# q in two shifted copies, turned in 32x32 blocks on VectorE: one attention and mixture-of-depths kernel, before and after

## The chip, the cores and the metric

The kernel runs on one core of one Trainium2 chip. The metric is the device time of one execution in microseconds. Before the change three runs gave 207.98, 209.22 and 209.74 us; their median, 209.22 us, is the time before. A profiled execution is a separate run of its own: it took 210.15 us, of which the span from the first to the last instruction is 208.4 us.

## What is computed

The reference has two parts. The first is linear attention over 8 batches, 8 heads, 576 tokens and a head size of 64, all in fp32:

```
q_s = softmax(q) over the 64 features of a token
k_s = softmax(k) over the 576 tokens
kv  = k_s^T v                    # 64 x 64 for each batch and head
x   = q_s kv                     # heads put side by side: 576 x 512 for each batch
```

The second part scores each token (`x . w_gate`), takes the 128 best of each batch, sends them through `relu(xe w1) w2` (512 to 1024 to 512), and adds the result, times the sigmoid of the score, to these rows. All other rows of the output are x itself.

## The kernel before, in words

**Units.** A unit is one batch and four heads, so there are 16 units, two for each batch. Each unit loads q, k and v (0.59 MB each), takes exp of q and k, sums `kv` over the tokens (`kv_mm`, line 310, made ready by `kv_out`), turns q (`q_t`, line 349) and multiplies (`x_mm`, line 375). A token's own softmax sum is one more column of that product. `x_sums` takes its reciprocal and a column with the score, `x_scale` writes the scaled rows into `xs`, and `x_store` writes them to the output.

**How q lies.** A partition holds nine neighbouring tokens: partitions 0 to 63 those of heads 0 and 2, partitions 64 to 127 those of heads 1 and 3 (heads 0 and 2 make one pair, 1 and 3 the other). The product needs the features on the partitions, so `q_t` turns q on TensorE: one transpose takes 64 tokens by two heads, and 18 of them turn a unit, ten in `q_t(u, 0)` (token rows 0 to 4 of each partition) and eight in `q_t(u, 1)` (rows 5 to 8). They land in PSUM, and one copy on ScalarE and one on VectorE (lines 356 and 354) take them to `qT`. Units 0 to 2 use a wider form, nine transposes of 128x128 (line 342).

**Rows of x.** `x_mm(u, 0)` makes the rows of the first pair of heads, `x_mm(u, 1)` those of the second, in five rounds each. A round writes token rows 0 to 4 to partitions 0 to 63 and rows 5 to 8 to partitions 64 to 127. There are nine rows, so the fifth round has real results for the lower partitions alone; the upper ones are filled with bf16 products of ones (line 367), so that the sums and the scale can run over all 128 partitions.

**The second part.** When both units of a batch are done, `score` and `score_row` make a row with all scores, `compare` (line 446, five times, on VectorE) counts for each token how many tokens score higher, `hits` marks the ranks below 128, `find` (line 473) turns the marks into row numbers, and `fetch` gathers these rows of x from the output by an indirect DMA on POOL (line 487). `turn` (line 524) transposes them, `mlp1` (line 544) and `mlp2` (line 554) are the two dense products in eight pieces each, `finish` adds, and `put` scatters the rows back (line 559).

**The order of work.** Everything is issued in an order written out by hand. After a start of its own, the loop has one step `s` per unit. A step handles unit `s` to its store, sums `kv` of unit `s + 1`, takes exp of q of unit `s + 1` and of k of unit `s + 2`, copies v of unit `s + 2`, and puts eight MLP pieces between these: odd steps `mlp1`, even steps `mlp2`, for an earlier batch. Each engine works through its own queue in that order. In even steps the search (`find`, `fetch`) comes after one MLP piece (two in step 16; in step 4 it stands further back), and `turn` stands before the last piece.

**Queues.** Loads and stores go through SP's queue: in step `s` the store of unit `s`, then k, v and q of unit `s + 3`, each into one of three buffers. The first load of a step waits for the last product of `x_mm(s, 1)`. A hardware DMA also waits, in the built program, for the landing of the one that was issued eight before it. Gathers and scatters go through POOL.

Of the kernel before, what the change touches and what calls it, by code (L numbers as in the profile page):

```python
# [8 lines left out]
F32 = mybir.dt.float32  # L9
# [8 lines left out]
def kernel(  # L18
# [34 lines left out]
    SD = S * D  # L53
    NQ = H // 4
    C = D + 2
    G = 2 * R
    LOW = 2.0 ** -30
    FAR = 2.0 ** 100
    UP = 2.0 ** 24
# [29 lines left out]
    def part(i):  # L89
        return slice(64 * i, 64 * i + 64)  # L90
# [10 lines left out]

    LD = 3
    FLAT = 0, 1
    RR = 4 * R
    raw = {w: [const.tile([P, 2 * T if w == "q" else RR, D], F32, name=f"{w}{n}") for n in range(LD)] for w in "qkv"}

    def view(t, paired):
        return t.rearrange("p (h r) d -> p h r d", h=4) if paired else t[:, :2 * T].rearrange("p (i r) d -> p i r d", i=2)
# [6 lines left out]
    def load(u, which, after=None, split=False, flat=False):  # L115
        b, qd = units[u]
        for what in which:
            src = {"q": q, "k": k, "v": v}[what]
            first = src[place(b), 4 * qd].offset
            dmas = []  # L120
            if flat:
                t = view(raw[what][u % LD], False)
                if split:
                    for h, queue in enumerate((nc.scalar, nc.sync)):
                        dmas.append(queue.dma_start(out=t[:, h].rearrange("p r d -> p (r d)"),
                                                    in_=bass.AP(tensor=src.tensor, offset=first + 2 * h * SD,
                                                                ap=[[T * D, P], [1, T * D]])))
                else:
                    dmas.append(nc.sync.dma_start(out=t.rearrange("p i r d -> p i (r d)"),  # L129
                                                  in_=bass.AP(tensor=src.tensor, offset=first,  # L130
                                                              ap=[[T * D, P], [2 * SD, 2], [1, T * D]])))
            elif what == "q":
                t = view(raw[what][u % LD], False)
                for r0, r1 in ROWS:
                    dmas.append(nc.sync.dma_start(out=t[:, :, r0:r1].rearrange("p i r d -> p i (r d)"),  # L135
                                                  in_=bass.AP(tensor=src.tensor, offset=first + r0 * D,
                                                              ap=[[T * D, P], [2 * SD, 2], [1, (r1 - r0) * D]])))
            else:
                t = view(raw[what][u % LD], True)
                for n, rows in ((1, N2), (0, R)):  # L140
                    dmas.append(nc.sync.dma_start(out=t[n::2, :, :rows].rearrange("p h r d -> p h (r d)"),  # L141
                                                  in_=bass.AP(tensor=src.tensor, offset=first + n * R * D,
                                                              ap=[[T * D, 64], [SD, 4], [1, rows * D]])))
            if after is not None:
                behind(dmas[0], after)
                after = None
        return dmas[-1]

    ROWS = (0, R), (R, T)
    ctx.enter_context(tc.manual_schedule())  # L150
    load(0, "k", split=True, flat=True)
    load(0, "vq", flat=True)
# [30 lines left out]
    ones_f = const.tile([P, 4 * P], F32, name="ones_f")  # L183
# [23 lines left out]
    for n in range(2):  # L207
# [6 lines left out]
    qrec = const.tile([P, NU, 2, G], F32, name="qrec")  # L214
    krec = const.tile([P, NU, 2], F32, name="krec")


    order_minus_p = const.tile([P, RP], F32, name="order_minus_p")
# [52 lines left out]
    def q_exp(u, c):  # L271
        if c == 0:
            st["qe", u] = at.tile([P, T, 2, D], F32, tag="qe", name="qe")
        r0, r1 = ROWS[c]
        qr = raw["q"][u % LD].rearrange("p (i r) d -> p r i d", i=2)
        nc.scalar.activation(out=st["qe", u][:, r0:r1], in_=qr[:, r0:r1], func=AF.Exp)  # L276

    def v_copy(u, engine=nc.scalar):
# [44 lines left out]
        nc.vector.reduce_sum(out=kw[:, :, D + 1], in_=prod, axis=AX.X)  # L323


    copies = []

    def q_t(u, c, on_vector=False, wide=False, later=False):
# [29 lines left out]
    def x_mm(u, a, wide=False, tag="x"):  # L358

        qT = st["qT", u] if a == 0 else st.pop(("qT", u))  # L360
        x = pair(tag, 2 if tag == "x" else 1)
        kw = kv_w[u % 2]
        for r in range(R):
            for i, c in QUARTERS:
                to = x[part(c), i, r * C:(r + 1) * C]
                if r == N2 and c:
                    last = nc.tensor.matmul(out=to, lhsT=ones_b[part(i), :D], rhs=ones_b[part(i), :C], start=True, stop=True)
                    continue
                if wide and r < N2:
                    if c == 0:  # L370
                        nc.tensor.matmul(out=x[:, i, r * C:(r + 1) * C],
                                         lhsT=qT[part(i), a, r].rearrange("p c t -> p (c t)"), rhs=kw[part(i), a],
                                         start=True, stop=True)
                    continue
                nc.tensor.matmul(out=to, lhsT=qT[part(i), a, r, c], rhs=kw[part(i), a], start=True, stop=True)  # L375
        st["x", u, a] = x[:, :, :R * C].rearrange("p i (r c) -> p i r c", r=R)
        return last

    xs, sr = {}, {}

    def x_sums(u, a):
        b, qd = units[u]
        if qd == 0 and a == 0:
            xs[b] = xp.tile([P, R, NQ, 2, 2, D], F32, tag="xs", name="xs", bufs=3)
            sr[b] = md.tile([P, NQ * 2, G], F32, tag="sr", name="sr")
        rec = qrec[:, u, a].rearrange("p (i r) -> p i r", i=2)
        out_s = sr[b][:, 2 * qd + a].rearrange("p (i r) -> p i r", i=2)
        x = st["x", u, a]
        nc.vector.reciprocal(out=rec, in_=x[:, :, :, D])
        nc.vector.tensor_mul(out_s, x[:, :, :, D + 1], rec)  # L390

    def x_scale(u, a):
        b, qd = units[u]
        rec = qrec[:, u, a].rearrange("p (i r) -> p i r", i=2)
        nc.vector.tensor_mul(xs[b][:, :, qd, :, a].rearrange("p r i d -> p i r d"), st.pop(("x", u, a))[:, :, :, :D],  # L395
                             rec.to_broadcast([P, 2, R, D]))

    def x_out(u, a):
        x_sums(u, a)
# [11 lines left out]
    def score(b, up=2):  # L411

        raw_s = s_all[:, b]
        nc.vector.reduce_sum(out=raw_s, in_=sr.pop(b).rearrange("p n (i r) -> p r n i", i=2), axis=AX.XY)
# [77 lines left out]
    def select(b, n, r):  # L492

        k0, m = slots[n]
        if r == 0:
            st["select", n] = bank("mm", 2), md.tile([P, R, P], F32, tag="hit_f", name="hit_f", bufs=1)
        t_ps, hit = st["select", n]
        far = md.tile([P, P], F32, tag="far", name="far")
# [147 lines left out]

    def in_range():

        rq, rk = qrec.rearrange("p u i n -> p (u i n)"), krec.rearrange("p u n -> p (u n)")
# [96 lines left out]
    for s in range(LAG, NU + LAG):  # L746
# [5 lines left out]
        def pieces(n, to=None):  # L752
            nonlocal f_next
            for _ in range(n if to is None else max(0, to - f_next)):
                each(piece, mlp_b, f_next)
                f_next += 1
# [72 lines left out]
            pieces(1)  # L829
        else:  # L830
            if chosen is not None and s not in AFTER:
                pieces(1 if here else 2)
                search()
            if here:
                q_t(s, 0)
                q_t(s, 1, on_vector=s > LAG + 1)
            if follows:
                kv_mm(s + 1)
                kv_out(s + 1)
# [73 lines left out]
```

## Time and profile before

| what | us |
|---|---|
| median of three runs (207.98 to 209.74) | 209.22 |
| profiled execution | 210.15 |
| its span | 208.4 |
| TensorE busy | 193.6 (93%) |
| VectorE busy | 119.0 (57%) |
| ScalarE busy | 92.1 (44%) |
| POOL busy | 32.4 (16%) |

The DMA engines moved 46.66 MB in the span. The page of the profile gives busy time by engine, the span in 40 slices of 5.2 us (a digit is the busy share in tenths), the chain of work that ended last, and groups of instructions by line. In a group, the number after `x` is how many there were, then come busy time in us, mean duration of one in ns, and after the last bar how long the engine was idle just before them and who ended that. The chain of waits is followed back from the last instruction: at each step to what released it, or to the instruction ahead of it on its engine. What is on the chain sets the time; what isn't on it has some slack.

### The profile page before, as it was taken

The page shows a single profiled execution, that of the slowest core. Times are in us where ns is not written, and L with a number is a line of the kernel's source. Part 1 is how long each engine was busy: PE and PEld are TensorE (multiplying, and loading weights), DVE is VectorE, ACT ScalarE, POOL GpSimd, SP SyncE. Part 2 cuts the span into 40 slices and gives each one's busy share as a digit, 9 for nine tenths or more (in the row PEclk, how much of TensorE's full clock was granted, in tenths as well). Part 3 has the DMA queues.
Part 4 walks back from the last instruction along what each step waited for, and adds up shares of the span by engine and source line. Part 5 has one row for each costly group of instructions (what it writes and reads, how often), then busy time and mean ns, then how long its engine had stood idle before and what let it go on. Part 6 is the DMA issues. An engine that isn't in the chain of part 4 may idle for free.

```text
span 208.4 us, 6943 instructions
## 1 busy us (share of the span) xinstructions
PE 193.6 (93%) x2955; PEld 148.8 (71%) x2955; DVE 119.0 (57%) x361; ACT 92.1 (44%) x135; POOL 32.4 (16%) x93
## 2 busy tenths in 40 slices
PE   7899799798989999999999999999999999999960
PEld 3486789785579848985698759974898579659520
DVE  6668735597167645776378717862776537714010
ACT  3468876574526624545434813672464022111100
POOL 5103000202010101210120104010211012126010
PEclk9999999999999999999999999999999999999995
DMA  6999999999786999995989779895880433131101
GB/s 218 397 307 330 384 360 372 371 381 329 193 296 158 309 327 250 283 279 170 233 282 253 231 175 304 212 314 129 256 247 4 103 110 74 48 101 53 58 5 53
DMA packets 37720, 46.66 MB, mean 224 GB/s; under 512 B 2353, under 2 KB 33073, under 8 KB 37682
## 3 DMA queue, kind: packets, MB, share of 16 engines
q1 hardware_dynamic: 36256, 41.66, 65.2%
q0 software_dynamic: 1280, 4.20, 5.7%
q8 instruction: 25, 0.41, 0.8%
q10 hardware_dynamic: 146, 0.30, 0.5%
q14 instruction: 13, 0.11, 0.2%
HBM read 34.61 MB, written 11.53 MB: 221 GB/s over the span
## 4 chain that ended last, share of the span: by engine, by line
PE 74%; DMA 16%; SPq 3%; issue 1%; ACT 1%; DVE 1%; POOL 0%; POOLq 0%; ACTq 0%
PE mm L544 25%; PE mm L554 25%; DMA k<-in_k_dram 15%; PE x L375 8%; PE kv L310 8%; PE x L349 4%; DMA xr<-out_dram,idx 2%; SPq L141 2%; PE kv L432 2%; PE mm L524 2%; SPq L135 1%; ACT ke L268 1%; PE mm L473 1%; SPq L169 0%; SPq L129 0%
## 5 line engine op out<-in xcount | busy, mean ns | idle before, releaser
L544 PE MATMUL mm<-xT,w 128*128 128x128 f32 x512 | 62.0, 278 | 0.3 <-DVE xT L532 0.3
L544 PEld LDWEIGHTS mm<-xT,w 128*128 128x128 f32 x512 | 58.8, 192 | 2.0 <-ACT xT L532 0.6
L554 PE MATMUL mm<-w,hT 128*128 128x512 f32 x128 | 59.3, 599 | 0.0
L446 DVE SCALAR_TENSOR_TENSOR junk<-srow,s,not_before 128x576 bf16<-128x576 f32 x40 | 32.7, 819 | 9.4 <-ACT srow L438 8.1
L554 PEld LDWEIGHTS mm<-w,hT 128*128 128x128 f32 x128 | 22.6, 190 | 20.6 <-issue 20.1
L567 DVE SCALAR_TENSOR_TENSOR o<-mm,g,xr 128x512 f32<-128x512 f32 x7 | 5.3, 751 | 35.6 <-PE mm L554 35.6
L395 DVE TENSOR_TENSOR xs<-x,qrec 128x640 f32<-128x640 f32 x31 | 24.1, 815 | 0.0
L375 PE MATMUL x<-kv_w,qT 64*64 64x66 f32 x1084 | 21.9, 222 | 1.7 <-issue 1.5
L268 ACT ACTIVATE ke<-k 128x1280 f32<-128x1280 f32 (+1 forms) x16 | 20.0, 1253 | 4.6 <-DMA k<-in_k_dram 4.6
L276 ACT ACTIVATE qe<-q 128x640 f32<-128x640 f32 (+1 forms) x32 | 20.1, 676 | 3.3 <-DMA q<-in_q_dram 3.3
L375 PEld LDWEIGHTS x<-kv_w,qT 64*64 64x64 f32 x1084 | 19.4, 134 | 3.0 <-issue 2.0
L310 PE MATMUL kv<-v_ones,ke 128*64 128x65 f32 x560 | 19.4, 224 | 1.1 <-ACT srow L438 1.1
L310 PEld LDWEIGHTS kv<-v_ones,ke 128*64 128x64 f32 x560 | 17.5, 137 | 2.3 <-ACT srow L438 1.3
L547 ACT ACTIVATE hT<-mm 128x512 f32<-128x512 f32 x16 | 9.6, 597 | 21.5 <-PE mm L544 21.5
L281 ACT COPY v_ones<-v 128x1280 f32<-128x1280 f32 x14 | 17.6, 1257 | 0.7 <-DMA v<-in_v_dram 0.4
L532 ACT COPY xT<-mm 128x512 f32<-128x512 f32 x7 | 4.1, 585 | 30.1 <-PE mm L524 30.1
L487 POOL DMA_INDIRECT xr<-out_dram,idx x8 | 8.3, 1036 | 53.4 <-PE x L349 22.6
L559 POOL DMA_INDIRECT out_dram<-o,idx x7 | 7.0, 996 | 58.9 <-DVE o L567 58.9
L356 ACT COPY qT<-x 128x640 f32<-128x640 f32 (+1 forms) x17 | 11.4, 682 | 9.5 <-PE x L349 8.7
L438 ACT ACTIVATE srow<-kv 128x576 f32<-128x576 f32 x7 | 4.5, 648 | 23.0 <-PE kv L432 23.0
L349 PEld LDWEIGHTS x<-ident,qe 64*128 64x128 f32 x234 | 8.3, 138 | 4.9 <-ACT xT L532 4.5
L354 DVE COPY qT<-x 128x512 f32<-128x512 f32 x11 | 7.6, 692 | 5.8 <-PE x L349 5.8
(115 smaller groups left out, 165.7 us busy)
## 6 DMA issues: line engine op xcount, KB each, us to landing
out_dram<-xs SPq DMA_DIRECT2D x16, 320.0 KB, 3.6
k<-in_k_dram SPq DMA_DIRECT2D x14, 320.0 KB, 5.1
v<-in_v_dram SPq DMA_DIRECT2D x14, 320.0 KB, 6.1
q<-in_q_dram SPq DMA_DIRECT2D x14, 320.0 KB, 6.2
w<-in_moe_w_dram SPq DMA_DIRECT2D x8, 512.0 KB, 7.6
out_dram<-xs SPq DMA_DIRECT2D x16, 256.0 KB, 4.3
k<-in_k_dram SPq DMA_DIRECT2D x14, 256.0 KB, 4.8
v<-in_v_dram SPq DMA_DIRECT2D x14, 256.0 KB, 4.7
```

What stands on the lines that cost most here:

```text
L268: nc.scalar.activation(out=ke, in_=view(raw["k"][u % LD], u not in FLAT), func=AF.Exp)
L276: nc.scalar.activation(out=st["qe", u][:, r0:r1], in_=qr[:, r0:r1], func=AF.Exp)
L281: engine.copy(out=out_v, in_=in_v)
L310: nc.tensor.matmul(out=kv_ps[part(i), a, :D + 1], lhsT=ke[:, 2 * i + a, r], rhs=vo[:, 2 * i + a, r], start=(r == 0), stop=(r == N2))
L349: nc.tensor.transpose(out=src[:, a, r], in_=qe[part(a), r0 + r].rearrange("p i d -> p (i d)"), identity=ident[part(a), part(a)])
L356: nc.scalar.copy(out=to, in_=src)
L375: nc.tensor.matmul(out=to, lhsT=qT[part(i), a, r, c], rhs=kw[part(i), a], start=True, stop=True)
L395: nc.vector.tensor_mul(xs[b][:, :, qd, :, a].rearrange("p r i d -> p i r d"), st.pop(("x", u, a))[:, :, :, :D], rec.to_broadcast([P, 2, R, ...
L446: nc.vector.scalar_tensor_tensor(junk, st["srow", b], st["s", b][:, r:r + 1], not_before[:, r], op0=OP.subtract, op1=OP.is_ge, accum_out=s ...
L544: st["piece"] = nc.tensor.matmul(out=h_ps[:, f % 4 * m:(f % 4 + 1) * m], lhsT=w1[:, d, f * P:(f + 1) * P], rhs=xT[:, d, :m], start=(d == 0 ...
L547: nc.scalar.activation(out=hT[:, f - 3:f + 1, :m], in_=h_ps[:, :4 * m].rearrange("p (f c) -> p f c", f=4), func=AF.Relu)
L554: st["piece"] = nc.tensor.matmul(out=st["y", b, n][:m], lhsT=st["hT", b, n][:, f, :m], rhs=w2[:, f], start=(f == 0), stop=(f == KF - 1))
```

## The change

For units 5 to 15 q is loaded by four DMAs of 32 partitions each instead of two of 128. Each partition receives 18 neighbouring tokens of each of two heads. Partition groups 0 and 1 read the same tokens, the second one shifted by 32 features (128 bytes); groups 2 and 3 do so for the other two heads. So the first 32 features of every 64 in a partition are the lower half of the features in groups 0 and 2 and the upper half in groups 1 and 3. Every value of q is read from memory twice, and only half of what lands is used: `q_exp` takes exp of that half (two times 576 elements per partition), and the new `q_blocks` turns it on VectorE in blocks of 32x32, straight into `qT` in SBUF. `q_t` no longer runs for these units, nor do its copies. The blocks of unit `s + 1` are turned in step `s`: in even steps both after the exp, in odd steps one ahead of the rank comparisons and one after `hits`.

The fifth round of `x_mm` moves to `x_mm(u, 0)` as a whole, with the fifth rows of both pairs (the second pair's on the upper partitions), in all units; `x_mm(u, 1)` has four rounds, and the products of ones go. `x_sums` and `x_scale` each get one small operation for those 64 partitions, and run over four rows instead of five for the second pair. Buffers whose unused halves are read are cleared at the start.

The search of the even steps comes after two MLP pieces instead of one. Some small buffers (`ones_f`, `order_minus_p`, `hit_f`, `far`) move into the second half of the q buffers, which became twice as large.

```diff
-    raw = {w: [const.tile([P, 2 * T if w == "q" else RR, D], F32, name=f"{w}{n}") for n in range(LD)] for w in "qkv"}
+    TWICE = range(5, NU)
+    raw = {w: [const.tile([P, 4 * T if w == "q" else RR, D], F32, name=f"{w}{n}") for n in range(LD)] for w in "qkv"}
...
+            elif what == "q" and u in TWICE:
+                t = raw[what][u % LD].rearrange("p (a n) d -> p a (n d)", a=2)
+                for g in range(4):
+                    dmas.append(nc.sync.dma_start(out=t[32 * g:32 * g + 32, :, :ROW],
+                                                  in_=bass.AP(tensor=src.tensor,
+                                                              offset=first + g // 2 * 2 * SD + g % 2 * D // 2,
+                                                              ap=[[2 * T * D, 32], [SD, 2], [1, ROW]])))
...
+    ROW = 2 * T * D - D // 2
...
+        if u in TWICE and u not in FLAT:
+            half = raw["q"][u % LD].rearrange("p (a n) (h s) -> p a n h s", a=2, h=2)[:, c, :, 0]
+            to = st["qe", u].rearrange("p r i d -> p (r i d)").rearrange("p (a n s) -> p a n s", a=2, n=2 * T)
+            nc.scalar.activation(out=to[:, c], in_=half, func=AF.Exp)
+            return
...
+    def q_blocks(u, a):
+        if u not in TWICE:
+            return
+        if a == 0:
+            st["qT", u] = at.tile([P, 2, R, 2, D], F32, tag="qT", name="qT")
+        to = st["qT", u].rearrange("p a r c d -> p a (r c d)")[:, :, :T * D].rearrange("p a (j t e) -> p a e j t", j=T, e=2)
+        qe = st["qe", u].rearrange("p r i d -> p (r i d)").rearrange("p (a e j s) -> p a e j s", a=2, e=2, j=T)
+        nc.vector.transpose(out=to[:, a], in_=qe[:, a])
...
-                if r == N2 and c:
-                    last = nc.tensor.matmul(out=to, lhsT=ones_b[part(i), :D], rhs=ones_b[part(i), :C], start=True, stop=True)
+                if r == N2:
+                    if a == 0:
+                        rows = by_token[part(i), c, r] if u in TWICE and u not in FLAT else qT[part(i), c, r, 0]
+                        last = nc.tensor.matmul(out=to, lhsT=rows, rhs=kw[part(i), c], start=True, stop=True)
                     continue
...
+        if a == 0:
+            nc.vector.tensor_mul(sr[b % 2][part(0), 2 * qd + 1, :, N2], x[part(1), :, N2, D + 1], qrec[part(1), u, 0, :, N2])
...
+        if a == 0:
+            nc.vector.tensor_mul(xs[b][part(0), N2, qd, :, 1], x[part(1), :, N2, :D],
+                                 qrec[part(1), u, 0, :, N2].to_broadcast([P // 2, 2, D]))
...
-                pieces(1 if here else 2)
+                pieces(2)
                 search()
-            if here:
+            if here and s not in TWICE:
                 q_t(s, 0)
-                q_t(s, 1, on_vector=s > LAG + 1)
+                q_t(s, 1)
...
+            if follows:
+                q_blocks(s + 1, 0)
+            if ends is not None:
                 ranks()
+            else:
+                q_blocks(s + 1, 1)
...
             if ends is not None:
                 each(hits, ends)
+                q_blocks(s + 1, 1)
```

More of the change, by code (lines that the diff above doesn't have):

```diff
@@ L55 @@
     C = D + 2
-    G = 2 * R
     LOW = 2.0 ** -30
@@ L103 @@
     FLAT = 0, 1
+    TWICE = range(5, NU)
     RR = 4 * R
-    raw = {w: [const.tile([P, 2 * T if w == "q" else RR, D], F32, name=f"{w}{n}") for n in range(LD)] for w in "qkv"}
+    raw = {w: [const.tile([P, 4 * T if w == "q" else RR, D], F32, name=f"{w}{n}") for n in range(LD)] for w in "qkv"}
+    spare = {n: raw["q"][n].rearrange("p r d -> p (r d)")[:, 2 * T * D:] for n in range(LD)}
     def view(t, paired):
@@ L182 @@
     w_ps = bank("mm", 2)
-    ones_f = const.tile([P, 4 * P], F32, name="ones_f")
+    ones_f = spare[2][:, :4 * P]
     nc.gpsimd.memset(ones_f, 1.0)
@@ L213 @@
         kv_w.append(t)
-    qrec = const.tile([P, NU, 2, G], F32, name="qrec")
+    for n in range(LD):
+        nc.gpsimd.memset(spare[n][:, ROW:], 0.0)
+    qrec = const.tile([P, NU, 2, 2, R], F32, name="qrec")
+    nc.gpsimd.memset(qrec, 1.0)
     krec = const.tile([P, NU, 2], F32, name="krec")
-    order_minus_p = const.tile([P, RP], F32, name="order_minus_p")
+    order_minus_p = spare[2][:, 4 * P:4 * P + RP]
     nc.gpsimd.iota(order_minus_p, pattern=[[1, RP]], base=0, channel_multiplier=-1,
@@ L273, in q_exp @@
             st["qe", u] = at.tile([P, T, 2, D], F32, tag="qe", name="qe")
+        if u in TWICE and u not in FLAT:
[3 more added lines that the diff above has]
+            return
         r0, r1 = ROWS[c]
-        qr = raw["q"][u % LD].rearrange("p (i r) d -> p r i d", i=2)
+        qr = raw["q"][u % LD][:, :2 * T].rearrange("p (i r) d -> p r i d", i=2)
         nc.scalar.activation(out=st["qe", u][:, r0:r1], in_=qr[:, r0:r1], func=AF.Exp)
@@ L360, in x_mm @@
         qT = st["qT", u] if a == 0 else st.pop(("qT", u))
+        by_token = qT.rearrange("p a r c d -> p a (r c) d")
         x = pair(tag, 2 if tag == "x" else 1)
@@ L365, in x_mm @@
                 to = x[part(c), i, r * C:(r + 1) * C]
-                if r == N2 and c:
-                    last = nc.tensor.matmul(out=to, lhsT=ones_b[part(i), :D], rhs=ones_b[part(i), :C], start=True, stop=True)
+                if r == N2:
+                    if a == 0:
+                        rows = by_token[part(i), c, r] if u in TWICE and u not in FLAT else qT[part(i), c, r, 0]
+                        last = nc.tensor.matmul(out=to, lhsT=rows, rhs=kw[part(i), c], start=True, stop=True)
                     continue
-                if wide and r < N2:
+                if wide:
                     if c == 0:
-                        nc.tensor.matmul(out=x[:, i, r * C:(r + 1) * C],
+                        last = nc.tensor.matmul(out=x[:, i, r * C:(r + 1) * C],
                                          lhsT=qT[part(i), a, r].rearrange("p c t -> p (c t)"), rhs=kw[part(i), a],
@@ L374, in x_mm @@
                     continue
-                nc.tensor.matmul(out=to, lhsT=qT[part(i), a, r, c], rhs=kw[part(i), a], start=True, stop=True)
-        st["x", u, a] = x[:, :, :R * C].rearrange("p i (r c) -> p i r c", r=R)
-        return last
-    xs, sr = {}, {}
+                rows = by_token[part(i), a, R * c + r] if u in TWICE and u not in FLAT else qT[part(i), a, r, c]
+                last = nc.tensor.matmul(out=to, lhsT=rows, rhs=kw[part(i), a], start=True, stop=True)
+        n = R - a
+        st["x", u, a] = x[:, :, :n * C].rearrange("p i (r c) -> p i r c", r=n)
+        return last
+    xs = {}
+    sr = [const.tile([P, NQ * 2, 2, R], F32, name=f"sr{n}") for n in range(2)]
+    for t in sr:
+        nc.gpsimd.memset(t[part(1)], 0.0)
     def x_sums(u, a):
@@ L384, in x_sums @@
             xs[b] = xp.tile([P, R, NQ, 2, 2, D], F32, tag="xs", name="xs", bufs=3)
[L385 to L390, printed above, removed]
+            if b == 0:
+                nc.gpsimd.memset(xs[b][part(1), N2], 0.0)
+        x, n = st["x", u, a], R - a
+        nc.vector.reciprocal(out=qrec[:, u, a, :, :n], in_=x[:, :, :, D])
+        nc.vector.tensor_mul(sr[b % 2][:, 2 * qd + a, :, :n], x[:, :, :, D + 1], qrec[:, u, a, :, :n])
+        if a == 0:
+            nc.vector.tensor_mul(sr[b % 2][part(0), 2 * qd + 1, :, N2], x[part(1), :, N2, D + 1], qrec[part(1), u, 0, :, N2])
     def x_scale(u, a):
         b, qd = units[u]
-        rec = qrec[:, u, a].rearrange("p (i r) -> p i r", i=2)
-        nc.vector.tensor_mul(xs[b][:, :, qd, :, a].rearrange("p r i d -> p i r d"), st.pop(("x", u, a))[:, :, :, :D],
-                             rec.to_broadcast([P, 2, R, D]))
+        x, n = st.pop(("x", u, a)), R - a
+        nc.vector.tensor_mul(xs[b][:, :n, qd, :, a].rearrange("p r i d -> p i r d"), x[:, :, :, :D],
+                             qrec[:, u, a, :, :n].to_broadcast([P, 2, n, D]))
+        if a == 0:
+            nc.vector.tensor_mul(xs[b][part(0), N2, qd, :, 1], x[part(1), :, N2, :D],
+                                 qrec[part(1), u, 0, :, N2].to_broadcast([P // 2, 2, D]))
     def x_out(u, a):
@@ L413, in score @@
         raw_s = s_all[:, b]
-        nc.vector.reduce_sum(out=raw_s, in_=sr.pop(b).rearrange("p n (i r) -> p r n i", i=2), axis=AX.XY)
+        nc.vector.reduce_sum(out=raw_s, in_=sr[b % 2].rearrange("p n i r -> p r n i"), axis=AX.XY)
         s = md.tile([P, R], F32, tag="s", name="s")
@@ L495, in select @@
         if r == 0:
-            st["select", n] = bank("mm", 2), md.tile([P, R, P], F32, tag="hit_f", name="hit_f", bufs=1)
+            st["select", n] = bank("mm", 2), spare[1][:, :R * P].rearrange("p (r t) -> p r t", r=R)
         t_ps, hit = st["select", n]
-        far = md.tile([P, P], F32, tag="far", name="far")
+        far = spare[1][:, (R + r % 2) * P:(R + r % 2 + 1) * P]
         nc.scalar.activation(out=far[:, :m], in_=slot_no[:, k0:k0 + m], func=AF.Abs, scale=-1.0,
@@ L647, in in_range @@
     def in_range():
-        rq, rk = qrec.rearrange("p u i n -> p (u i n)"), krec.rearrange("p u n -> p (u n)")
+        rq, rk = qrec.rearrange("p u a i n -> p (u a i n)"), krec.rearrange("p u n -> p (u n)")
         sc = s_all.rearrange("p b r -> p (b r)")
```

## The prediction

> **What bounds the kernel now.** I read the forty slices first, then the chain of waits that ended last, then busy time by window, and last the groups of the operations the change touches.
>
> ```profile
> PE   7899799798989999999999999999999999999960
> DMA  6999999999786999995989779895880433131101
> ```
>
> TensorE and the DMA engines are both nearly full over the first 130 us, so the slices alone don't say which one sets the time. The chain does. Up to 39.70 us it runs through landings of k (15% of the span), from there through TensorE to 201.11 us, almost without a break. One turn of it, around an even unit (columns: start, us, what):
>
> ```profile
> 90.81 0.86 PE mm L554 x2
> 91.67 0.18 PE mm L473 x5
> 91.86 0.70 PE x L349 x18
> 92.56 1.32 PE kv L310 x40
> ...
> 95.20 5.35 PE mm L554 x12
> 100.55 0.44 PE mm L524 x4
> 100.99 0.86 PE mm L554 x2
> 101.85 0.71 PE x L349 x18
> ```
>
> Every piece ends where the next begins. L349 is the turning of q (`q_t`): 0.70 us per unit, on the path. Two units take 113.95 - 91.67 = 22.3 us. Now how full the DMA engines are beside that (columns: busy us and instructions of PE, PEld, DVE, ACT, POOL; granted clock; DMA share; GB/s):
>
> ```profile
> 42.00:50.00 8.00, 7.34 (x179) 5.79 (x176) 7.04 (x24) 4.39 (x9) 0.65 (x1) 1.00 1.07 377
> 74.00:76.00 2.00, 2.00 (x6) 0.81 (x6) 1.24 (x4) 0.66 (x1) 0.00 (x0) 1.00 1.04 367
> 88.00:89.00 1.00, 1.00 (x12) 1.00 (x11) 0.96 (x3) 1.00 (x1) 0.00 (x0) 1.00 0.95 213
> 84.90:107.00 22.10, 22.10 (x363) 17.27 (x361) 13.90 (x41) 10.81 (x15) 3.21 (x9) 1.00 0.83 241
> ```
>
> Over two units the DMA engines are busy 0.83 x 22.1 = 18.3 us, and idle 3.8 us. They can be busy at very different rates: 377 GB/s with a deep queue of loads, about 200 where a store of x runs by itself (88 to 89 us).
>
> [...]
> - [...] `x_store` takes 64 neighbouring partitions and runs at 203 to 213 GB/s alone, while k and v, on every second partition, come at 377. [...] at 74 to 76 us two stores stand back to back behind q and 367 GB/s are reached. No transfer of before covers 32 partitions.
> - [...] No run here shows a transpose; the trace's slope for VectorE comes from the rows below.
> [...]
>
> **The change part by part.**
>
> *`q_t` of units 5 to 15 goes.* 18 transposes, 0.70 us on the chain, eleven times: -7.7 us if nothing else becomes late. Its two copies go as well: 0.69 us each on ScalarE (off the path, worth nothing) and on VectorE.
>
> ```profile
> L395 DVE TENSOR_TENSOR xs<-x,qrec 128x640 f32<-128x640 f32 x31 | 24.1, 815 | 0.0
> L356 ACT COPY qT<-x 128x640 f32<-128x640 f32 x15 | 10.4, 692 | 9.5 <-PE x L349 8.7 <-PE x L342 0.7
> L354 DVE COPY qT<-x 128x512 f32<-128x512 f32 x11 | 7.6, 692 | 5.8 <-PE x L349 5.8
> L320 DVE TENSOR_TENSOR kv_w<-kv,krec 128x128 f32<-128x128 f32 x16 | 4.7, 292 | 0.6
> ```
>
> *`q_blocks` comes.* Two VectorE transposes per unit, 128x576 each. From L395 and L320, VectorE pays (815 - 292) / 512 = 1.02 ns per element, so 576 elements are about 815 - 65 = 750 ns. [...] upper end 1.35 us [...]; I take 0.75. Per unit VectorE gains 1.5 and loses 0.69. In even steps both lie behind `x_scale`, where VectorE idles for 4 us before the finish. In odd steps the first stands ahead of the five rank comparisons, which today wait 1.07 us for the score row (idle before L446 at 86.24): that covers it, at 1.35 us it costs some 0.5. The second stands behind the hits, ahead of the small sums that make the indices of the gather; the search, one MLP piece (0.86 us) later, covers it. The ranks queue behind a transpose that waits for the exp of q: if q lands late, the ranks are late too.
>
> *Exp.* Two of 576 instead of 640 and 512: the same 1152 elements, zero.
>
> *x in one round.* 36 fp32 products and 4 bf16 ones become 36; on the chain the four (L367) show 0.02 us per unit. VectorE gains two small operations (about 0.17 us by the 10-element row and 0.23 by the 128-element one) and its second scale is 128 elements shorter (-0.13): +0.3 us per unit, in idle time. Sum on the path: -0.3 us over 14 units. If the idle time were gone it would delay the ranks by 0.3 us.
>
> *Loads of q.* Each unit now moves 4 x 32 x 2 x 4480 = 1,146,880 bytes instead of 589,824: +0.557 MB, 6.1 MB for eleven units. Four issues instead of two cost SP 2 x 0.51 = 1.0 us per unit; SP issues for 5 to 7 us of 11, so that is free unless the queue is full: in the built order each load waits for the landing of the one eight issues earlier, and a unit now has ten. Bounds for one q: at 377 GB/s 3.0 us (+1.5), at the 200 GB/s of the isolated store 5.7 us (+4.1). Below zero it can't go, the bytes are more. I take +2.0, a rate of about 320 GB/s: the pieces follow each other in a queue that the change keeps deep, like the stores at 74 us.
>
> *Initial clears.* Some 1.3 us of POOL before 5 us; the chain waits for k until 9.57 us. Zero.
>
> **Sum.** TensorE alone needs 22.3 - 1.5 = 20.8 us per two units. The DMA engines need 18.3 + 2 x 2.0 = 22.3, less what stores save in a deep queue (0.59 MB at 205 GB/s is 2.9 us, at 367 1.6, so up to 1.3 each; I take 0.7, twice): 20.9. That is a tie with TensorE. So nearly the whole 8.0 us is left over the span, less short waits where a store or gather comes late; I take 2.5 us for them (about 0.5 at each of five batches). Against the profiled execution, 210.15 us (span 208.4 and 1.75 around it): 210.15 - 8.0 + 2.5 = 204.65. That execution was 0.9 us above the median of the three runs; against 209.22 it is 203.7 us.
>
> **The rivals.**
> 1. *The loads of q become the bound (slower).* Place: SP's queue, q ahead of the next `x_store`, k and v. Price: +4.1 us per unit at 200 GB/s. Then two units need 18.3 + 8.2 - 1.4 = 25.1 us against 22.3 now: +1.4 per unit, 14 over ten units, less some 6 us by which loads now land ahead of use (q of unit 10 is in by 97 us and its exp starts at 102.99), less the 2 us of `q_t` after the last load: +6, 215 us. It turns slower where the extra cost passes (22.3 + 1.4 - 18.3) / 2 = 2.7 us, a rate of q under 270 GB/s. For it: 32 neighbouring partitions, and the isolated stores. Against: 367 GB/s at 74 us.
> 2. *The gather is late (no gain).* Today the search ends at 91.85, rows gathered from 92.52 land 4.9 us later at 97.4, and the turning of xr starts at 100.55: 3.1 us spare. The change takes 0.70 (no `q_t` between) and 0.86 (search later) from that: 1.6 us are left. Landings vary:
>
> ```profile
> DMA to landing us min/median/max: 3.3/4.8/7.4
> ```
>
> The 7.4 is the one at 70.2 us, in a full stretch. If all are like it, and the store they wait for is late as well, 1 to 1.5 us are lost at each of six batches: 203.7 - 2.5 + 7.5 = 208.7 us. For it: the stretch gets fuller. Against: xr is only 0.26 MB, and the period stretches with each wait.
> 3. *Transposes at 1.35 us.* Ranks and hits are late by 0.5 to 0.8 us in five odd steps: +3, 206.5 us. It is still faster.
>
> **Chances.** Likeliest case 0.40, transposes dear 0.10 (together the faster side, with a little from rival 2: 0.52), rival 2 0.16, rival 1 0.34. Differences of 1% (2.1 us) are about what a measurement of this kernel can tell from none. Faster 0.52, same 0.14, slower 0.34. With no waits at all it is 201.2; leaving out about one in ten above, rival 1 reaches to 217. Range 201 to 217; the likeliest case's own is 201 to 206.5.
>
> **What would show it.** Right: L349's counterpart has 36 transposes for units 3 and 4; two units on the chain are 20.8 to 21.2 us; transposes near 750 ns; q's four transfers land within 4 us of the first issue in full stretches; DMA share near 1.0 at over 290 GB/s until about 145 us. Rival 1: GB/s near 200 while q moves, TensorE waiting at `kv` or `x` for k or q, the last load well after 155 us. Rival 2: TensorE idle ahead of L524's counterpart, put down to xr. A wait for a reason not named here, such as transposes of 2 us, would make all of it wrong.

## The result and the profile after

The changed kernel takes 226.24 us (median of 4, 222.91 to 230.56), the kernel before beside it 208.87 us. The ratio is 1.071, with a 95% interval from 1.061 to 1.082: the change makes the kernel slower. (A ratio compares the least disturbed executions of both, so it is below the quotient of the two medians.) I had said 203.7 us. The profiled execution after took 222.91 us, its span is 221.1 us; the span before was 208.4.

First the forty slices of after, now 5.5 us each, with the granted clock between the two lines shown of before:

```profile
PE   7998999796089994999959994999699999999960
PEclk9999999999658999799999999999999999999996
DMA  6999999999995999999999999999999052431101
```

TensorE now has holes (the 0 in slice 11, then a 4, 5, 4 and 6, a period of four to five slices), and its clock falls in or behind the first two of them. The DMA line has lost its holes but for one slice (66 to 72 us): it is full until 171 us. Work that TensorE gave up is not what the kernel waits for any more.

The chain of waits of after, through two even steps (start, us, what; pieces under 0.4 us are left out):

```profile
51.73 9.70 DMA xr<-out_dram,idx
61.56 1.09 PE mm L563 x4
62.65 1.71 PE mm L593 x2
64.36 2.36 PE kv L328 x40
...
76.19 1.72 PE mm L593 x4
78.68 9.07 DMA xr<-out_dram,idx
87.88 1.03 PE mm L563 x4
...
101.40 1.72 PE mm L593 x4
103.89 8.76 DMA xr<-out_dram,idx
```

Before, the chain had TensorE pieces end to end here. Now each turn of it holds the gather of `fetch` (line 526) from issue to landing, 9 us, and then `turn` (L563). The counterpart of L349 is gone, as predicted. The waits of after, by engine, with us in all, times, and the longest, say who pays:

```profile
PE mm L563 <- DMA xr<-out_dram,idx: 19.1, 6, 8.3
ACT ke L281 <- DMA k<-in_k_dram: 6.9, 3, 2.9
ACT v_ones L299 <- DMA v<-in_v_dram: 6.4, 5, 2.5
```

Busy time by window of after (the columns as before: PE, PEld, DVE, ACT, POOL, then clock, DMA share, GB/s):

```profile
52.00:54.00 2.00, 1.24 (x3) 0.19 (x1) 0.79 (x2) 0.38 (x1) 0.92 (x1) 1.00 1.03 200
54.00:56.00 2.00, 0.00 (x0) 0.00 (x0) 0.00 (x0) 0.89 (x1) 0.00 (x0) 1.00 1.10 190
58.00:60.00 2.00, 0.00 (x0) 0.00 (x0) 0.00 (x0) 0.67 (x1) 0.00 (x0) 0.50 1.02 319
82.00:84.00 2.00, 2.00 (x6) 0.81 (x5) 1.94 (x6) 0.25 (x1) 0.00 (x0) 1.00 1.02 221
86.00:88.00 2.00, 0.12 (x1) 0.15 (x2) 0.00 (x0) 0.00 (x0) 0.00 (x0) 0.99 1.08 374
```

The DMA share is 1.0 in all of them, but the rate is 190 to 221 GB/s while q moves and 374 when it is through. So the queue is deep and q is still slow: at 221 GB/s the 1.147 MB of a unit take 5.2 us, against 1.6 us for 0.59 MB at 377 before. At 58 us the clock is 0.50 after TensorE has stood still since 53.2 us. It halves 4.0 us into this stop and stays so until 67.48 us, so that `kv_mm` at 64.36 takes 2.36 us instead of 1.32. It also halved behind a stop of 2.9 us (85.0 to 87.9 us), and not behind three later ones of 2.1 to 2.9 us.

The transposes on VectorE, and the scale of x, in the groups of after (mean ns before the last bar):

```profile
L351 DVE STREAM_TRANSPOSE qT<-qe 128x576 f32<-128x576 f32 x22 | 16.2, 759 | 0.0
L431 DVE TENSOR_TENSOR xs<-x,qrec 128x640 f32<-128x640 f32 (+1 forms) x31 | 23.5, 757 | 0.3
```

One transpose is 759 ns; I had taken 750, from VectorE's slope in other operations of before. And the landing of the gather (`DMA to landing`, from the view of the tile `xr`), 4.8 us in the middle before:

```profile
DMA to landing us min/median/max: 3.4/8.2/9.7
```

**Where the time goes.** `turn` starts once per batch, two units apart. From the timelines of several kernels, the start of the first one and the distances to the next, in us (labels are those of the experiments below):

| kernel | first | | | | | | last |
|---|---|---|---|---|---|---|---|
| before | 54.75 | 23.36 | 22.28 | 22.28 | 22.27 | 22.28 | 18.00 |
| after | 61.56 | 26.32 | 24.90 | 24.14 | 22.84 | 20.98 | 17.19 |
| q once, two rounds (e10) | 53.99 | 22.62 | 20.82 | 20.84 | 20.94 | 20.85 | 17.23 |
| even units (e6) | 57.75 | 25.86 | 25.10 | 26.68 | 26.19 | 22.37 | 18.02 |
| odd units (e16) | 57.31 | 24.09 | 21.58 | 21.49 | 21.67 | 21.41 | 17.21 |
| even units' q behind (e18) | 62.68 | 24.35 | 23.82 | 24.87 | 25.69 | 27.04 | 17.15 |
| odd units from 9 (e21) | 54.25 | 22.89 | 22.05 | 21.34 | 21.34 | 21.72 | 17.07 |

After against before: +6.81 at the first, +8.01 over the next four, -2.11 over the last two, when only the last unit's q is still to be loaded (its issues begin at 161.14 us): +12.71, the 12.7 us between the spans. I predicted 20.8 us for two units on TensorE. The last full distance of after is 20.98.

### The profile page after: what moved, and what is told of

It reads as the page before. It is cut to its first block, busy times and chain, and to the rows that moved or that the text cites. A ratio compares the mean times of both kernels' runs of the same rounds, so it can differ in the third digit from the quotient of the medians.

```text
span 221.1 us, 6483 instructions
## 1 busy us (share of the span) xinstructions
PE 189.8 (86%) x2691; PEld 143.1 (65%) x2693; DVE 134.3 (61%) x404; ACT 85.7 (39%) x124; POOL 34.7 (16%) x100
## 4 chain that ended last, share of the span: by engine, by line
PE 51%; DMA 32%; DVE 8%; issue 2%; ACT 1%; POOL 1%; SPq 0%; POOLq 0%; ACTq 0%; DVEq 0%
PE mm L583 23%; DMA xr<-out_dram,idx 21%; PE mm L593 13%; DMA k<-in_k_dram 11%; PE kv L328 4%; PE x L406 4%; PE mm L563 2%; DVE junk L485 2%; PE kv L471 1%; PE kv L323 1%; DVE not_before L271 1%; DVE xs L431 1%; ACT ke L281 1%; PE x L401 1%; PE x L397 0%
## 5 line engine op out<-in xcount | busy, mean ns | idle before, releaser
L593 PE MATMUL mm<-w,hT 128*128 128x512 f32 x128 | 61.1, 614 | 0.0
L593 PEld LDWEIGHTS mm<-w,hT 128*128 128x128 f32 x128 | 23.1, 195 | 20.5 <-issue 19.8
L431 DVE TENSOR_TENSOR xs<-x,qrec 128x640 f32<-128x640 f32 (+1 forms) x31 | 23.5, 757 | 0.3
L328 PEld LDWEIGHTS kv<-v_ones,ke 128*64 128x64 f32 x560 | 18.8, 146 | 7.0 <-ACT xT L571 2.3
L328 PE MATMUL kv<-v_ones,ke 128*64 128x65 f32 x560 | 20.8, 233 | 1.1 <-ACT srow L477 1.1
L563 PE MATMUL mm<-ident,xr 128*128 128x128 f32 x28 | 5.4, 321 | 19.1 <-DMA xr<-out_dram,idx 19.1
L406 PE MATMUL x<-kv_w,qT 64*64 64x66 f32 x960 | 19.8, 224 | 0.1
L563 PEld LDWEIGHTS mm<-ident,xr 128*128 128x128 f32 x28 | 3.6, 159 | 24.5 <-issue 24.4
L406 PEld LDWEIGHTS x<-kv_w,qT 64*64 64x64 f32 x960 | 17.4, 136 | 1.3 <-issue 0.2
L586 ACT ACTIVATE hT<-mm 128x512 f32<-128x512 f32 x16 | 9.6, 597 | 21.4 <-PE mm L583 21.4
L337 DVE RECIPROCAL krec<-kv 128x2 f32<-128x2 f32 x16 | 2.7, 170 | 23.9 <-PE kv L328 23.2
L351 DVE STREAM_TRANSPOSE qT<-qe 128x576 f32<-128x576 f32 x22 | 16.2, 759 | 0.0
```

Source lines behind the costliest of these rows:

```text
L328: nc.tensor.matmul(out=kv_ps[part(i), a, :D + 1], lhsT=ke[:, 2 * i + a, r], rhs=vo[:, 2 * i + a, r], start=(r == 0), stop=(r == N2))
L351: nc.vector.transpose(out=to[:, a], in_=qe[:, a])
L406: last = nc.tensor.matmul(out=to, lhsT=rows, rhs=kw[part(i), a], start=True, stop=True)
L431: nc.vector.tensor_mul(xs[b][:, :n, qd, :, a].rearrange("p r i d -> p i r d"), x[:, :, :, :D], qrec[:, u, a, :, :n].to_broadcast([P, 2, n, ...
L563: nc.tensor.transpose(out=t_ps[:, d * m:(d + 1) * m], in_=xr[:m, d * P:(d + 1) * P], identity=ident[:m, :m])
L586: nc.scalar.activation(out=hT[:, f - 3:f + 1, :m], in_=h_ps[:, :4 * m].rearrange("p (f c) -> p f c", f=4), func=AF.Relu)
```

## The experiments

In each I compare by the ratio to the kernel before, which ran beside it: 208.9 to 209.4 us in most cases, 212.3 and 212.5 us on the chip where e1 to e4 and e6, e7, e11 and e15 ran.

**Partitions or bytes (e1, e2, e3).** The first edit keeps every byte and transfer but spreads the 32 rows over every fourth partition; the second keeps the 32 neighbours and halves the rows; the third loads q once, over 128 partitions. Values of q then lie at other places, or old ones are used.

```
e1: -  dma_start(out=t[32 * g:32 * g + 32, :, :ROW], ...)
    +  dma_start(out=t[g::4, :, :ROW], ...)
e2: +  dma_start(out=t[32 * g:32 * g + 32, :, :ROW // 2], ... ap=[[2 * T * D, 32], [SD, 2], [1, ROW // 2]])
e3: +  for c0, c1 in ((0, 5 * D), (5 * D, ROW // 2)):
    +      dma_start(out=t[:, :, c0:c1], ... ap=[[T * D, P], [2 * SD, 2], [1, c1 - c0]])
```

> The changed kernel, but each of q's four transfers goes to every fourth partition instead of 32 neighbours: the same number of transfers, bytes and rows, the values of q on other partitions (so the part of q that each block gets is changed, and the output with it). Theory A (32 neighbouring partitions take data at about 205 GB/s only, whatever the depth of the queue, and this makes the DMA engines the bound): q moves at 330 to 380 GB/s, the waits for gathered rows shrink from 19 us to under 6, time 202 to 208 us. Theory B (the 6.1 MB more, ten instead of eight transfers per unit): no change, 221 to 230 us.

> The changed kernel with q's four transfers on the same 32 neighbouring partitions, each row cut to half (the rest of q's buffer is cleared and old values, so part of q is left out). The bytes of q are those of before, 0.57 MB per unit. Theory A: q at 205 GB/s takes 2.8 us instead of 1.6 before; with 3.8 us idle in two units before, that nearly fits: 203 to 210 us. Theory B (bytes alone): as e3, within 1%, 200 to 204 us.

> The changed kernel with q loaded once, 0.57 MB in two transfers over 128 partitions as before; VectorE still transposes 2 x 576 elements, half of them from cleared or old values (part of q is left out). Theories A and B, by which only q's loads cost: TensorE's gain alone is left, 200 to 204 us. Theory C (the search one piece later and the transposes ahead of the ranks make the gather late by themselves): over 207 us, with TensorE waiting for gathered rows.

Measured: e1 211.85 us, ratio 0.995 (0.992 to 0.998); e2 210.70 us, 0.989 (0.986 to 0.992); e3 206.96 us, 0.976 (0.969 to 0.982). The wait of `turn` for gathered rows in e1, 19.1 us in after:

```profile
PE mm L563 <- DMA xr<-out_dram,idx: 4.2, 3, 3.6
```

The same bytes on other partitions take away the whole loss: from 1.071 to 0.995 it is 7.6%, 16 us. In the traces' packet records, one row of q (4480 bytes) takes 0.31 us on average in after and 0.19 us in e1; sixteen engines at that pace move about 230 and 380 GB/s. But half the bytes on the same 32 neighbours take it away as well (e2). So the loss needs both, the neighbouring partitions and the doubled bytes. It fits that what counts is the time for which q holds the engines: estimated from 221 and 377 GB/s, it is 5.2 us per unit in after, 3.0 in e1, 2.6 in e2 and 1.5 in e3. Against the loss either edit suffices; the bytes added cost 1.9% (e1 to e3), the partitions alone 1.3% (e2 to e3). But all three lie above what I had expected of them, so a part of the gain was missing too (more on that under e10).

**Two queues (e4).** Groups 0 and 1 from SP's queue, groups 2 and 3 from ScalarE's; the output is the full one.

```
-  for g in range(4):
-      nc.sync.dma_start(...)
+  for g in (0, 2, 1, 3):
+      queue = nc.sync if g < 2 else nc.scalar
+      queue.dma_start(...)
```

> The changed kernel, with the transfers to partitions 0 to 63 in SP's queue and those to 64 to 127 in ScalarE's, so that both halves can be on their way at the same time. Theory A with the two queues taking turns: q at over 300 GB/s, 204 to 212 us, less if ScalarE isn't held up by the waits of its two transfers. If transfers to the halves don't overlap even so: 221 to 230 us.

Measured: 234.25 us, ratio 1.106 (1.099 to 1.114), worse than after. The waits of e4:

```profile
ACT ke L282 <- DMA k<-in_k_dram: 29.3, 8, 10.1
ACT v_ones L300 <- DMA v<-in_v_dram: 21.5, 9, 4.6
```

Now k and v are late, and ScalarE, which also issues, waits for them. By the packet records q's rows from SP's queue and those from ScalarE's were at no time on their way together, so whether the two halves would run side by side from two queues stays untested. What made e4 worse is that ScalarE's issues and its other work hold each other up, as far as these waits tell.

**Another order in one queue (e5).** The four transfers in the order 0, 2, 1, 3, so that neighbours in the queue go to different halves of the partitions; the output is the full one.

> The four transfers of q stay as they are, but follow each other in the order group 0, 2, 1, 3 instead of 0, 1, 2, 3; the output is the full one. Theory A1 ([...] a transfer to the other half of the partitions can run beside it once it stands next in the queue): 205 to 214 us, and over 300 GB/s while q moves. Theory A2 (each transfer is held to its own rate whatever stands next to it): as the changed kernel, 221 to 230 us, about 200 GB/s while q moves.

Measured: 223.92 us, ratio 1.059 (1.051 to 1.067), against 1.071 for after. It points to a gain of 1%, but the intervals overlap: near what A2 said, and nothing like A1. The packet records show that the gain is there: a row of q takes 0.27 us on average instead of 0.31. (With e11 and e15, below, the same edit is clear.)

**The loads alone (e8).** The kernel before, with only the loads of q from unit 5 on taken from the change, and the larger buffers that they need (the values of q lie at other places).

> The kernel before, with the changed kernel's loads of q from unit 5 on and nothing else of the change that matters: q is still turned on TensorE (with values at other places), the fifth rows stay in two rounds, the search stays after one piece. Theory A (the loads of q to 32 neighbouring partitions alone make the loss, as the gather and k and v stand behind them): 221 to 234 us, the turning of gathered rows waits over 10 us in all for the gather. Theory B (the loss needs the order of the changed kernel: the later search, or the work moved to VectorE): 208 to 214 us.

Measured: 228.47 us, ratio 1.093 (1.088 to 1.098); `turn` waits 11.3 us for the gather, which is on the chain with 17% (2% before, 21% in after). Theory A: the loads alone make the loss, whatever the search and VectorE do. The rest of the change takes 2% of it back.

**The search (e7).** The changed kernel with the search back after one MLP piece.

```
-  pieces(2)
+  pieces(1 if here else 2)
   search()
```

> The changed kernel with the search back after one MLP piece, nothing else. Theory A (the gather's bytes stand behind the slow loads of q, wherever the search is): 223 to 231 us, no gain of more than 1 per cent on the changed kernel, and the gather takes longer to land instead. Theory B (the later search makes the gather late): 214 to 219 us, with the waits for the gathered rows down from 19 us to under 10 us.

Measured: 228.13 us, ratio 1.068 (1.059 to 1.077), as after. `turn` still waits 16.9 us, and the gather takes 8.9 us in the middle instead of 8.2. The later search is not the cause.

**What the rest of the change does (e9, e10).** e9 is the kernel before with the fifth rows of both pairs in one round and nothing else. e10 is e3 (q once) with the fifth rows back in two rounds, to find out why e3 gained less than I expected. Some steps of e3's trace had a pause of TensorE of 0.4 to 0.6 us at the fifth round.

```
e9:  -  TWICE = range(5, NU)
     +  TWICE = range(NU, NU)          # none; q_t and the search as before
e10: +  if r == N2 and c:              # e3, with ones on the upper partitions in both rounds
     +      last = nc.tensor.matmul(out=to, lhsT=ones_b[part(i), :D], rhs=ones_b[part(i), :C], start=True, stop=True)
     +      continue
```

> The fifth rows of both pairs in one round of x, in all units, and nothing else: q is loaded once and turned on TensorE, the search stays after one piece. Theory A (the fifth round itself brings the pauses of 0.4 to 0.6 us per unit that the run with q loaded once showed in it): 210 to 214 us, 1 to 2.5 per cent over the kernel before, with pauses of TensorE at the fifth round in eight or more steps. Theory B (as I predicted, it changes TensorE by 0.02 us per unit): 208 to 210 us, within 0.5 per cent of the kernel before.

> The run with q loaded once (two transfers over 128 partitions, rest of the buffer old values) with the fifth rows put back into two rounds of x, as in the kernel before. Theory A (the fifth round in one takes back most of what the missing transposes save): 200 to 204 us. Theory B (the pauses come with the way q is turned and its wait, whatever the order of the rounds): 205.5 to 208 us, as with one round.

Measured: e9 211.28 us, ratio 1.004 (0.999 to 1.009); e10 202.81 us, ratio 0.971 (0.967 to 0.974). In e10 two units take 20.8 to 20.9 us (table), what I had worked out for TensorE. This is its chain (start, us, what), whose counterpart before had L349 between L544's and L310's pieces:

```profile
109.47 1.72 PE mm L585 x4
111.19 0.11 PE mm L504 x5
111.30 1.32 PE kv L327 x40
112.62 0.64 PE x L403 x33
```

So without the slow loads the 7.7 us of `q_t` come out nearly whole: 2.9% of 209.35 is 6.2 us, and the profiled spans differ by 8.1. That the fifth round makes the pauses was a false trail. They go with the chip, not with the rounds: all runs on the one where the kernel before takes 212 us have pauses of 0.3 to 0.6 us in the products of x after 60 us, in most units that VectorE turns, with one round (e1 to e4, e6, e7) and with two (e11, e15). In after, e5, e16, e18 and e21, which have one round and ran where the kernel before takes 209 us, there are none there. The eight or nine pauses in each of e1, e2 and e3 make 3.2 to 3.6 us, and these runs lie 0.7 to 3.9 us above what I had expected. What makes the pauses stays open. e9's trace has one pause, of 1.9 us; but for that and the first, its distances over two units are 22.04 us, before 22.28.

**Which units (e6, e11, e15).** The loads and the turning in the even units 6 to 14 alone. I took these loads to be away from the gather. e11 is e6 with the fifth rows in two rounds, e15 is e11 with the order 0, 2, 1, 3. The output of these and all later runs is the full one.

```
e6: -  TWICE = range(5, NU)
    +  TWICE = range(6, NU, 2)
```

> The changed kernel with its loads and 32x32 turning of q in units 6, 8, 10, 12 and 14 alone (the other units as before); the output is the full one. These loads are issued in odd steps, away from the store and the gather of the even steps. Theory A (the slow loads do harm where they meet the gather; five units save 0.70 us each): 204 to 207 us. Theory B (each slow load costs the DMA queues about 1.5 us that come out at the end anyway): 211 to 217 us.

> The same, with the fifth rows back in two rounds of x as before. Theory A (the fifth round in one costs TensorE 0.5 us or more in the units turned by VectorE): 1 to 3 us less than the run with one round. Theory B (no difference, as the prediction had it): within 1 us of it.

> The same as the run before it (even units, fifth rows in two rounds) with the four transfers in the order group 0, 2, 1, 3. If neighbouring transfers overlap a little, as the run with this order in all units hinted (3 us there for eleven units): 0.5 to 1.5 us less; if not, the same within 0.5 us.

Measured: e6 225.74 us, ratio 1.062 (1.058 to 1.067); e11 224.35 us, 1.053 (1.047 to 1.059); e15 219.36 us, 1.032 (1.027 to 1.038). Here both theories fell: five slow loads cost nearly as much as eleven. SP's queue in e6 shows why (start of the issues, us from the first to the last, line, transfers):

```profile
71.98 1.97 SPq L137 DMA_DIRECT2D q<-in_q_dram  x4
73.99 7.71 SPq L444 DMA_DIRECT2D out_dram<-xs  x6
...
97.15 1.96 SPq L137 DMA_DIRECT2D q<-in_q_dram  x4
```

and its chain has the gather right after each:

```profile
74.78 8.69 DMA xr<-out_dram,idx
...
99.06 9.52 DMA xr<-out_dram,idx
```

The q of an even unit is issued at the end of the odd step before, 2 to 3 us ahead of the gather. I had it the wrong way round. The order 0, 2, 1, 3 is worth 2% here: transfers to different halves ran somewhat faster when they followed each other (a row of q took 0.28 us on average, in e11 0.31). (That e11 is 1% below e6 isn't borne out below: e21 against e20 goes the other way.)

**Place or amount (e16, e17, e18, e19).** e16 is e6 with the odd units 5 to 15 instead. Their q is issued in even steps, after the gather. e17 is e16 with the search after one piece and the fifth rows in two rounds, e19 is e17 with the order 0, 2, 1, 3. e18 has all eleven units, with the q of even units one step later.

```
e16: +  TWICE = range(5, NU, 2)
e18: -  QUEUE = {"odd": "x+0 kv+3 q+3", "even": "x+0 kv+3 q+3", 5: "x+0 kv+3 q+3 x-5 x-4"}
     +  QUEUE = {"odd": "x+0 kv+3", "even": "x+0 q+2 kv+3 q+3", 5: "x+0 kv+3 x-5 x-4"}
```

> As the run with the even units, but with units 5, 7, 9, 11, 13 and 15. Their loads of q are issued at the end of the even steps, behind the gather, where those of the even units stand at the end of the odd steps, right ahead of the store and the gather of the next step. Theory A (a slow load does harm by standing ahead of the gather; behind it it is hidden): 204 to 209 us at a before of 209 us, ratio under 1.0. Theory B (each slow load costs the queue its own time wherever it stands): as with the even units, ratio 1.05 to 1.07.

> Odd units alone, the fifth rows in two rounds and the search after one piece as in the kernel before: only what gains is left of the change. Theory A: six units by 0.70 us on TensorE less, 204 to 206 us at a before of 209 us, ratio 0.976 to 0.988. Theory B: ratio over 1.03.

> The changed kernel, all eleven units, with the q of even units loaded one step later, behind the store and ahead of k and v of the next even step, so that no slow load stands ahead of a gather that is issued after it. Theory A (place alone): 203 to 209 us. Theory B (place for the gather, but two slow loads of 5.5 us beside about 12.8 us of k, v and stores in two steps make 24 us, over TensorE's 21): 212 to 219 us, k and v late instead of the gathered rows. Theory C (amount alone): 222 to 230 us.

> The run with odd units, two rounds and the early search, with the four transfers in the order group 0, 2, 1, 3. With the even units this order gave 2 per cent, with the loads ahead of the gather. If the loads of odd units are hidden: no difference over 0.5 per cent to the run without it; if they still hold something up: 0.5 to 1.5 per cent less.

Measured: e16 210.77 us, ratio 1.008 (1.005 to 1.011); e17 209.55 us, 1.000 (0.996 to 1.003); e19 208.67 us, 0.993 (0.989 to 0.997); e18 230.17 us against 209.20 (lowest 224.79 against 207.82). The gather of e16:

```profile
DMA to landing us min/median/max: 3.4/4.4/6.0
```

Six loads behind the gather cost 5% less than five ahead of it, with the same edit otherwise. So place decides between even and odd. (The turning on VectorE, which also stands elsewhere in even and odd steps, isn't it: e10 bears it in all units.) The odd loads aren't free, though: e16 and e17 meet neither of their theories, and the 0.7% by which e19 is below e17 suggests that something still waits for these loads. And e18 doesn't save the kernel with all eleven: three of its four runs took 229.9 to 230.6 us. The waits in the trace, of one of the three:

```profile
ACT qe L290 <- DMA q<-in_q_dram: 40.5, 10, 9.0
PE mm L563 <- DMA xr<-out_dram,idx: 11.4, 4, 9.6
```

The gather is freed (9.6 of its 11.4 us are one wait), and q itself is late. That looks like the amount, but the trace speaks against it as the main reason. From 94 us on ScalarE waits 6.2 to 9.0 us for the q of each even unit and under 1 us for that of each odd one: it is ready for a moved load 1.4 to 2.9 us after the first of its four transfers is issued. The DMA share is 0.94 to 0.95 from 85 to 160 us, so the engines even have some slack. (The edit also loads q of unit 6 twice, 1.15 MB more.) So e18 trades one late transfer for another, and whether eleven units fit in a better order stays open.

An estimate of the amount: before, the DMA engines were busy 18.3 us over two units, of which two q at 377 GB/s are 3.1. With two q of 5.2 us each it is 15.2 + 10.4 = 25.6 us; with one, 15.2 + 1.6 + 5.2 = 22.0, close to TensorE's 21.6. The estimate is too high for the later steps: in after two units with two slow q pass in 22.8 us (137 to 160 us), with a DMA share of 1.02. But that is still over TensorE's 20.8, while one slow q can just be hidden if nothing waits behind it: in e16 the share is 0.94 (82 to 124 us).

e16 reaches 21.4 to 21.7 us for two units from the third column of the table on, one `q_t` less than before. Yet it gains nothing in all: 2.6 us are lost before the first `turn` and 0.7 in the next distance.

**Leaving the early loads out (e20, e21).** Units 9, 11, 13 and 15 alone, the search after one piece, the order 0, 2, 1, 3. e20 has the fifth rows in two rounds, e21 in one as the changed kernel.

```
-  TWICE = range(5, NU)
+  TWICE = range(9, NU, 2)
```

> Units 9, 11, 13 and 15 alone with loads twice and blocks, fifth rows in two rounds, search after one piece, transfers in the order group 0, 2, 1, 3. Theory A (the early loads, up to 81 us, ate the gain of the odd units): as the kernel before up to 78 us, then 21.57 us for two units, in all 4 times 0.71 us less: 2.8 us or a ratio of 0.987 (0.982 to 0.992). Theory B (the odd units lose elsewhere too): 0.993 to 1.003.

> The same with the fifth rows of both pairs in one round, in all units, as in the changed kernel. Theory A (the round in one saves about 0.1 us in a unit turned by TensorE, as the run with it alone showed between pauses, and costs 0.5 us in a unit turned by VectorE): the same as the run with two rounds within 0.7 per cent. Theory B (it always saves): 0.5 to 1 per cent less. Theory C (it always costs): 0.7 per cent or more above.

Measured: e20 206.49 us, ratio 0.989 (0.983 to 0.994); e21 204.81 us, 0.979 (0.974 to 0.985). e20 is what theory A said: 2.8 us less, 4 times 0.71. The early loads had eaten the gain: e19, which has those of units 5 and 7 besides, starts its first `turn` at 57.41 us, e20 at 54.44. e21 is lower by a further 1%: in it two units that TensorE turns take 22.05 us (third column), before 22.28, as in e9, so the one round is worth about 0.11 us per unit where no pause comes. The slices of e21:

```profile
PE   7689999879989999999999999999999999999960
PEclk9999999999999999999999999999999999999995
DMA  6999999999798999997799979995994344131101
```

TensorE has no hole from 61 us on, its clock stays up, and DMA has gaps again. e21 beats both kernels: 4.5 us below the kernel before in the medians, with the full output.

## Why the prediction was wrong

- **The failed step** is "I take +2.0, a rate of about 320 GB/s: the pieces follow each other in a queue that the change keeps deep, like the stores at 74 us". The analogy does not hold. In a deep queue q still comes at 190 to 221 GB/s, 3.6 us more per unit than before (5.2 - 1.6). Nor were the 367 GB/s those of stores: by the packet records the gather ran in these two microseconds, and so did the rest of a q that landed at 74.80 us; with the stores all but alone, from 76.5 to 79.5 us, the rate is 269. The upper bound, +4.1, was close; I chose the wrong end. My own rule said that it turns slower under 270 GB/s. Of the signs I had named, q was to land within 4 us; it lands in 5.4 to 9.9 us, 8.1 in the middle. Rival 1 had the price and two of its signs (near 200 GB/s, last load after 155 us: 161.14), and its 25.1 us for two units lie near the first half of after (26.3, 24.9, 24.1). But TensorE waits at `turn`, not at `kv` or `x`, and the rival's 215 us are 11 short.
- **The second failed step** is rival 2's "1.6 us are left". It reckoned with a landing of 4.9 us, and of 7.4 at worst. Beside q's loads the first five gathers take 7.8 to 9.7 us, and I didn't put the two rivals together: rival 1's bytes reach TensorE through rival 2's gather, and only in part through k and v. Moving the search was no part of it (e7).
- **Place.** I wrote of q "ahead of the next `x_store`, k and v" and not of the gather, which is issued 2 to 3 us behind the q of the even units. e6 against e16 shows that this place is worth 5%.
- **TensorE: right.** 0.70 us per unit on the chain, 20.8 us for two units: e10 shows 20.8 to 20.9, and the last distances of after show it once the loads are over.
- **Transposes: right**, 759 ns against 750, in idle time; e10 bears them without delay. Rival 3 didn't occur; its 1.35 us was a guess of mine that no trace of before showed.
- **x in one round: right in sign, low in size** where it runs undisturbed: about 0.11 us per unit (e21) against 0.02. Alone it can't be told from nothing (e9).
- **Waits, 2.5 us: mis-sized.** `turn` alone waits 19.1 us. Behind two of its waits the clock is 0.50, and the first work there takes up to twice its time (two products of L593 1.71 us, 0.86 at 113.54 us); I hadn't counted that.

## What to carry to other kernels

Price a transfer by the time it holds the DMA engines, which here depended on both the partitions it lands on and its bytes (1.071 in after, 0.995 and 0.989 with either changed), and don't take a rate from a transfer of another shape or direction because the queue is as deep. Then look at what is issued within a few microseconds behind it, on whatever queue: here a gather of 0.26 MB that landed behind slow loads stopped TensorE for 19.1 us in all, and with six such loads issued after it the kernel took 0.8% more than before (e16), with five ahead of it 6.2% (e6). When a change has a good half and a bad half, apply it only to the units whose transfers fit into the gaps.

## What the hardware showed that I had not expected

- Loads to 32 neighbouring partitions stayed near 200 GB/s (190 to 221) in a queue with DMA share 1.0, where k, v, stores and the gather together ran at 368 to 393 GB/s (84 to 92 us of after). A row of q took 0.31 us there, and 0.19 us in transfers of the same number and size to every fourth partition (e1).
- Two such transfers to different halves gained a little when they followed each other in one queue: a row of q took 0.28 us instead of 0.31, and the kernel 2% less (e15 against e11).
- A gather of 0.26 MB from POOL's own queue took 3.4 us at the end of after, when no more loads ran, and up to 9.7 us beside a full SP queue.
- The granted clock of TensorE fell to 0.50 behind a stop of 2.9 us (after, at 88 us) and stayed so until 3.5 us after work began again, or 5.9 us behind the stop of 8.3 us. In e9, behind a stop of 1.9 us (136.3 to 138.2 us), the slice from 140.7 us shows 0.7, and 12 products of L593 took 7.12 us instead of 5.42. Stops of 2.1 to 2.9 us later in after left the clock at 1.0.
